# Two hybrid layers on one core: weaving the last second product by fifths, a norm in two stages, weights loaded in pieces

## The chip, the core and the metric

The kernel runs on one core of a Trainium2 chip. The core has TensorE (PE, matmuls; PEld is its weight load), VectorE (DVE), ScalarE (ACT), GpSimd (POOL) and SyncE (SP), which here issues nearly all DMAs. The metric is the device time of one execution in microseconds, lower is better.

## The reference

Two pairs of a linear-attention layer and a dense layer run one after the other over x of shape 1 x 2048 x 576, in float32, with the same weights in both pairs:

```python
def _A_ref(x, wqkv, w_phi, wo):                 # H = 32 heads of Dh = 18
    qkv = (x @ wqkv) ...                        # q, k, v
    pq, pk = q @ w_phi, k @ w_phi               # per head
    phi_q = concat(softmax(pq), softmax(-pq)); phi_k = the same of pk
    kv = phi_k^T v;  z = sum of phi_k over the sequence
    o = (phi_q kv) / (phi_q z + 1e-6)
    return o @ wo
def _B_ref(x, w1, b1, w2, b2):                  # F = 4608
    return relu(x @ w1 + b1) ** 2 @ w2 + b2
for both pairs:
    x = x + _A_ref(layernorm(x), ...)
    x = x + _B_ref(layernorm(x), ...)
```

The sums kv and z go over the whole sequence, so no query of a layer can be finished before all keys of that layer are through.

## The kernel before

**Tiles.** The sequence is cut into four blocks of TB = 512 rows, each of NT = 4 tiles of 128. To keep float32's accuracy each operand of a large matmul is held as a high part (F32R, a rounded copy made on ScalarE) and a low part (what is left, subtracted on VectorE or GpSimd), and a product is the sum of three: high by high, high by low, low by high. A projection of one tile and one half of the 576 columns (`project`, L476 to 485) is 14 matmuls of 288 columns; `make_v` (L487) and `make_raw` do both halves of a tile one after the other. `kv_tile` (L558) adds a tile to the sums kv in 64 small matmuls (as the trace counts them) of 36 columns.

**Order of the work.** The program is Python that is traced; a planner then orders each engine's instructions by their place in the source and by when it thinks their inputs are ready, and takes buffers from pools. The kernel steers it by generators that `yield` costs: `weave(main, other, rate)` (L101) adds `rate` for every step of `main` and pays steps of `other` from it. `tc.issue_after(ins)` keeps what is traced inside it, on the engine of `ins`, behind `ins` in that engine's queue; it is an order and no wait. `held` (L668) and `chained` (L129) wrap generators in it: `chained` keeps each step's VectorE, ScalarE and GpSimd instructions behind those of the step before. Buffers matter too: work woven beside a product has two PSUM buffers (tag w), x tiles have five, weights of the kind q, k, v or o two for each part (whi, wlo).

**Stages.** `g_fold` (L233) folds w_phi into the q and k weights and splits the k and v weights (in its inner `times`, ScalarE and GpSimd split v's chunk c at L302 and L303 as soon as chunk c is folded). Keys and values of layer 0 follow. Then in each layer:

- `barrier` (L1384): the queries of two blocks, the end of the sums, and for the first block the features of its queries. `g_phi` (L715) goes tile by tile: products with z (`phi_products`, one on VectorE, one on GpSimd, L694), sums (L700), factors, scaling (L712). Two tiles are finished, tile 2's products are begun, and `g_out` (L743) is called with two parts: part 0 turns tiles 0 and 1 (L768) and multiplies them by kv (L784). The rest of `g_phi`, so tile 3's products too, comes behind the last subtraction of part 0 (L788). Then come the output projections (`x_after`, L794, matmuls at L805), part 1, and `g_norm`, which makes the normed and transposed input of the dense layer: `moments` (L370) computes statistics on VectorE (L375, L376) and the reciprocal root on GpSimd (L377, L378), `scale` applies them (L393, L394), and `transpose`, `split_main`, `transpose_rest`, `split_rest` (L404 to L426) turn tiles and split them. `keep` (L827) adds the second bias on GpSimd and stores the row tile.
- two blocks through `g_mlp` (L846), with the attention of other blocks woven in (`back_first` at rate 3.7, `back_second` at 5.0);
- the last two blocks as a pair in `g_pair`: `products` (w1, by a scheme with fewer block products) and one block's second product (w2); then `seconds` (L1339) does the other block's second product: per f of NF = 36, `by_rows` is 12 matmuls of 448 columns (L1231), `features` is 3 of 512 (L1221), with loads of w2 (L1188) and of the hidden rows hd (L1269) three f ahead. In layer 0 `back_keys` (L1496), the norm, v, k and sums of the next layer's first three blocks, is woven into `seconds` at rate 4.0. Its norm is `g_norm` with `fine=True`: four tiles scaled one after the other, 2.2 each, then turned and split.

Once split, a weight is stored to DRAM (`keep_split`) and later loaded as it is: `wloaded` (L354) loads both parts of a half at once by `moved` (L346); `wpair` takes both halves.

The stages that the change touches are the fold, the barrier, the loads of q and o, and `back_keys` inside `seconds`. The weave around `seconds` is this:

```python
        back = iter(()) if layer else chained(back_keys())
        for k, _ in enumerate(products):
            if k == NP - 1:
                next(back, None)
                next(back, None)
        weave(seconds, back, 4.0)
```

## Time and profile before

| | us |
|---|---|
| three timed runs: median (lowest to highest) | 2530.28 (2529.72 to 2532.84) |
| the profiled execution, its own time | 2538.57 |
| span of its instructions | 2536.8 |
| TensorE's mean granted clock over the span | 0.992 |

The profile comes from one execution, which took a little longer than the timed runs; its times count from the first instruction. Rows show instructions by line, engine and tile, the output's name before the arrow; buffer numbers are left out, and a block's number stands in the name: n_3, n_2 and n_0 are the norms that `back_keys` makes for blocks 3, 2 and 0 (and those names serve layer 0's norms too), w_3k0h is the high part of half 0 of the k weights loaded for block 3, t0 and t1 are the barriers of layers 0 and 1, m_pacacc and m_pach the sums of `seconds`. A row of waits names the waiting engine, tile and line, what it waited for, then the time in total, the number of waits, and the longest. Ends of matmuls are modelled, so the distance between starts says more than a matmul's own duration.

### The profile page before, as it was taken

To read this page: it belongs to the slowest core of one execution; us is meant where nothing else is said; L and a number is where in the kernel's file an instruction comes from. 1 tells how busy PE (TensorE), PEld (TensorE's weight loads), DVE (VectorE), ACT (ScalarE), POOL (GpSimd) and SP (SyncE) were. 2 spreads that over 40 slices of the span, in tenths; PEclk is the share of its full clock that TensorE was granted. 3 is DMA by queue.
4 is the path that set the end of the run, shared out by engine and by line. 5 is a ranking of instruction groups with operands and counts; after the bars stand their busy time and mean duration, and the time that the engine had idled before them with its cause. 6 is when DMAs were issued, how large, how long until landed. Compare 5 with 4: busy or idle time off the path is not lost.

```text
span 2536.8 us, 41468 instructions
## 1 busy us (share of the span) xinstructions
PE 2481.7 (98%) x15108; PEld 2179.8 (86%) x15108; DVE 1570.9 (62%) x2514; ACT 1265.5 (50%) x2245; POOL 949.5 (37%) x1101
## 2 busy tenths in 40 slices
PE   8998999999999999999999989999999999999999
PEld 8997888889888888888889988888898888888888
DVE  6778848554856655554667679394548566555444
ACT  4344545443446666663333435454445466666642
POOL 3544312212325555551333333031123355565322
PEclk8999999999999999999999999999999999999999
DMA  9222643356434433328654134333563444333363
GB/s 326 79 69 91 196 116 85 103 164 213 133 119 125 143 114 99 113 93 295 206 180 148 47 128 150 102 99 98 166 222 112 129 130 142 116 96 109 112 199 127
DMA packets 249691, 348.52 MB, mean 137 GB/s; under 512 B 30158, under 2 KB 157262, under 8 KB 246926
## 3 DMA queue, kind: packets, MB, share of 16 engines
q1 hardware_dynamic: 248228, 343.18, 42.7%
q8 instruction: 118, 1.93, 0.3%
q10 hardware_dynamic: 1258, 2.70, 0.3%
q14 instruction: 87, 0.71, 0.1%
HBM read 279.46 MB, written 66.32 MB: 136 GB/s over the span
## 4 chain that ended last, share of the span: by engine, by line
PE 47%; DVE 3%; DMA 2%; ACT 1%; POOL 1%; issue 1%; SPq 0%; DVEq 0%; ACTq 0%; POOLq 0%
PE m_1ph L887 5%; PE m_0ph L887 4%; PE m_pacacc L1231 4%; PE m_ppx L1202 4%; PE m_1acc L914 3%; PE m_0acc L914 3%; PE m_pacc L1231 3%; PE m_ppy L1202 2%; PE m_pacacc L1221 2%; PE m_pach L1231 1%; PE m_0acc L905 1%; PE m_1acc L905 1%; PE m_pacc L1221 1%; PE m_ppz L1202 1%; PE a_0po L805 1%
## 5 line engine op out<-in xcount | busy, mean ns | idle before, releaser
L1192 POOL TENSOR_TENSOR m_ps<-m_pr,m_ps 128x128 fp32r<-128x128 f32 x144 | 118.2, 821 | 338.6 <-ACT m_ps L1190 282.9
L1191 DVE TENSOR_TENSOR m_ps<-m_pr,m_ps 128x448 fp32r<-128x448 f32 x144 | 98.1, 681 | 194.7 <-ACT m_ps L1190 191.3
L1231 PE MATMUL m_pacc<-m_ps,m_phb 128*128 128x448 f32 x864 | 188.5, 366 | 0.0
L1231 PEld LDWEIGHTS m_pacc<-m_ps,m_phb 128*128 128x128 f32 x864 | 162.2, 188 | 18.0
L1190 ACT ACTIVATE m_ps<-m_pr 128x576 fp32r<-128x576 f32 x144 | 98.1, 681 | 154.5 <-issue 88.2
L1231 PE MATMUL m_pacacc<-m_ps,m_phc 128*128 128x448 f32 x648 | 147.7, 370 | 0.0
L1231 PEld LDWEIGHTS m_pacacc<-m_ps,m_phc 128*128 128x128 f32 x648 | 122.6, 190 | 9.9
L1212 DVE TENSOR_TENSOR m_phb<-m_pz,m_phb 128x512 fp32r<-128x512 f32 x72 | 56.5, 784 | 113.1 <-ACT m_pz L1211 111.6
L914 PE MATMUL m_2acc<-m_2s,m_2hb 128*128 128x448 f32 x432 | 100.2, 366 | 0.0
L914 PE MATMUL m_0acc<-m_0s,m_0hb 128*128 128x448 f32 x432 | 100.1, 366 | 0.0
L887 PE MATMUL m_3ph<-t0onh,m_3h 128*128 128x512 f32 (+1 forms) x380 | 98.0, 383 | 1.6 <-DVE t0onh L426 0.8
L914 PE MATMUL m_1acc<-m_1s,m_1hb 128*128 128x448 f32 x432 | 99.4, 365 | 0.0
L914 PE MATMUL m_3acc<-m_3s,m_3hb 128*128 128x448 f32 x432 | 99.4, 365 | 0.0
L887 PE MATMUL m_1ph<-t1onh,m_1h 128*128 128x512 f32 (+1 forms) x380 | 97.8, 382 | 1.5 <-DVE t1onh L426 0.8
L887 PE MATMUL m_0ph<-a_0nh,m_0h 128*128 128x512 f32 (+1 forms) x380 | 97.8, 384 | 0.0
L887 PE MATMUL m_2ph<-a_2nh,m_2h 128*128 128x512 f32 (+1 forms) x380 | 97.8, 384 | 0.0
L914 PEld LDWEIGHTS m_2acc<-m_2s,m_2hb 128*128 128x128 f32 x432 | 80.9, 188 | 10.5 <-ACT m_2hb L895 0.2
L914 PEld LDWEIGHTS m_0acc<-m_0s,m_0hb 128*128 128x128 f32 x432 | 80.9, 188 | 10.6 <-ACT m_0hb L895 0.2
L914 PEld LDWEIGHTS m_1acc<-m_1s,m_1hb 128*128 128x128 f32 x432 | 81.1, 188 | 10.3
L914 PEld LDWEIGHTS m_3acc<-m_3s,m_3hb 128*128 128x128 f32 x432 | 81.1, 188 | 10.3
L872 POOL TENSOR_TENSOR m_3s<-m_3r,m_3s 128x128 fp32r<-128x128 f32 x36 | 24.6, 683 | 168.6 <-ACT m_3s L867 154.1
L872 POOL TENSOR_TENSOR m_1s<-m_1r,m_1s 128x128 fp32r<-128x128 f32 x36 | 24.7, 686 | 167.7 <-ACT m_1s L867 153.3
(2440 smaller groups left out, 7372.1 us busy)
## 6 DMA issues: line engine op xcount, KB each, us to landing
m_pr<-in_B_w SPq DMA_DIRECT2D x144, 288.0 KB
m_pr<-in_B_w SPq DMA_DIRECT2D x72, 256.0 KB
hd<-m_pu SPq DMA_DIRECT2D x72, 256.0 KB
m_pg<-hd SPq DMA_DIRECT2D x72, 256.0 KB
m_3r<-in_B_w SPq DMA_DIRECT2D x36, 288.0 KB
m_2r<-in_B_w SPq DMA_DIRECT2D x36, 288.0 KB
m_1r<-in_B_w SPq DMA_DIRECT2D x36, 288.0 KB
m_0r<-in_B_w SPq DMA_DIRECT2D x36, 288.0 KB
```

The lines of the kernel that those rows point to most:

```text
L805: nc.tensor.matmul(pt[:, :HP], a, m[:w, g], start=(g == 0 and k == 0), stop=(g == NG - 1 and k == 2))
L872: nc.gpsimd.tensor_sub(s2[:, D + R : 2 * D], r2[:, R:], s2[:, R:D].bitcast(F32))
L887: dense["hidden"] = nc.tensor.matmul(ph[:, cols], a, m, start=(k == 0), stop=(k == len(ops) - 1))
L905: nc.tensor.matmul(acc[KC], a, m, start=(f == 0 and k == 0), stop=(f == NF - 1 and k == 2))
L914: nc.tensor.matmul(acc[t][:, :R], a[:, rows], m, start=(f == 0 and k == 0), stop=(f == NF - 1 and k == 2))
L1190: nc.scalar.activation(s2[:, :D], r2, AF.Copy)
L1191: nc.vector.tensor_sub(s2[:, D : D + R], r2[:, :R], s2[:, :R].bitcast(F32))
L1192: nc.gpsimd.tensor_sub(s2[:, D + R : 2 * D], r2[:, R:], s2[:, R:D].bitcast(F32))
L1202: nc.tensor.matmul(ps, a, m, start=start and i == 0, stop=i == len(ms) - 1, skip_group_check=True)
L1212: nc.vector.tensor_sub(hl, r, hh.bitcast(F32))
L1221: nc.tensor.matmul(accs[b][KC], a, m, start=(g == 0 and k == 0), stop=(g == NF - 1 and k == 2))
L1231: nc.tensor.matmul(accs[b][t][:, :R], a[:, rows], m, start=(g == 0 and k == 0), stop=(g == NF - 1 and k == 2))
```

## The change

- **By fifths, in TensorE's source order.** `seconds` yields after each tile's row matmuls and after the features, five times per f, and the rate is 0.85 (it was one yield at 4.0). `chained(..., strict=True)` also keeps each woven step's matmuls behind the last matmul traced before it.
- **The norm in two stages.** With `fine=True`, `begin` (the load and the statistics) of tile t+1 is a step of its own ahead of `scale` of tile t. Six such steps of the first block are taken before the last step of `products` ends (there were two steps of one tile each). The next block's first six are taken between the half projections of v.
- **Weights in pieces.** `g_load` issues one part of one half per step, each behind SyncE's last traced DMA. v is projected half by half (`half_v`) and k's halves are loaded after each; q and o are loaded in such steps too.
- **The barrier.** `g_phi` goes away: products and sums of tiles 2 and 3 are both traced before `g_out`, their GpSimd part behind GpSimd's last traced instruction. In `g_out` with two parts, the tail is written out: norm tiles 0 and 1 behind part 1's last subtraction, transposes behind named output projections, bias additions and stores behind the last needed root.
- **The fold.** v's chunk c is split when chunk c+1 is folded, the last two together.

```diff
-    def chained(gen):
+    def chained(gen, strict=False):
         ends, engines = {}, (nc.vector.engine, nc.scalar.engine, nc.gpsimd.engine)
         while True:
             traced = nc.cur_bb.bb.instructions
             mark = len(traced)
+            if strict:
+                ends[nc.tensor.engine] = traced_on(nc.tensor)
...
+            for c in ([c - 1] if i == 2 and c else []) + ([c] if i == 2 and c == KC else []):
                 for half in range(2):
                     hi, lo = (piece[:, c] for piece in vpair[half])
...
+    def g_load(which, half, name, into):
+
+        into[half] = piece_tiles(f"{name}{which}{half}", TAGS_A)
+        for p in range(2):
+            with tc.issue_after(traced_on(nc.sync)):
+                moved(which, half, into[half], False, (p,))
+            yield 1.0
...
-        for t in range(NT):
-            apart(t)
-            yield 2.2
-        yield from pipeline(3 * NT // 2, (cross, split), (0.3, 0.6))
+        yield from pipeline(NT, (start, apart), (2.0, 1.6))
+        yield from pipeline(3 * NT // 2, (cross, split), (0.3, 0.9))
...
+        scale, turn_rows, turn_rest = next(g_norm(xs_of.__getitem__, dst, f"{name}n", None, None))
...
+        with tc.issue_after(dense["part"].ins):
+            xns = [scale(t) for t in range(2)]
+        xs_of.append(x_after(2))
+        behind_out(turn_rows, 0, xns[0])
+        other = g_after(3)
+        next(other)
+        behind_out(turn_rows, 1, xns[1])
+        behind_out(turn_rest, 0)
+        xs_of.append(next(other))
+        xns.append(scale(2))
+        kept_rows(0, 1)
+        behind_out(turn_rows, 2, xns[2])
+        xns.append(scale(3))
+        kept_rows(2, 3)
+
+        def rest():
+            turn_rows(3, xns[3])
+            turn_rest(1)
...
-                second(f)
+                for t in range(NT):
+                    by_rows(f, [t], range(3))
+                    yield
+                features(f, range(3))
+                del high[f], wide[f]
                 yield
...
         def own():
-            yield from g_q(x, wpair("q", name), raws, name)
+            pair = {}
+            for half in range(2):
+                yield from g_load("q", half, name, pair)
+            yield from g_q(x, pair, raws, name)
...
-        next(phi)
+        with tc.issue_after(traced_on(nc.gpsimd)):
+            for t in range(2, NT):
+                add(t)
+        phi = (finish(t) for t in range(2, NT))
...
+                for n, cost in enumerate(norm):
+                    yield cost
+                    if n > 5:
+                        next(loads, None)
+                drain(loads)
...
                 if not last:
                     spill(b, xk)
-                    yield from paced(g_v(xk, wpair("v", f"w{m}"), vts, f"v{m}"), 1.0)
-                pair = wpair("k", f"w{m}")
+                    norm = norm_of(order[i + 1])
+                    vts = [next_slot() for _ in range(NT)]
+                    for half in range(2):
+                        for t in range(NT):
+                            half_v(xk, t, wv[half], half, vts[t], f"v{m}")
+                            yield 0.5
+                            if len(ahead) < 6:
+                                ahead.append(t)
+                                yield next(norm)
+                        yield from paced(g_load("k", half, f"w{m}", wk), 0.3)
+                    ahead.clear()
...
                 yield from pipeline(NT, (raw, start, lambda t: soft_exp(es[t]), end, keep_sums),
-                                    (1.0, 2.6, 0.4, 1.8, 0.8))
+                                    (0.5, 2.4, 0.4, 2.0, 0.8))
...
-        back = iter(()) if layer else chained(back_keys())
+        back = iter(()) if layer else chained(back_keys(), True)
         for k, _ in enumerate(products):
             if k == NP - 1:
-                next(back, None)
-                next(back, None)
-        weave(seconds, back, 4.0)
+                for _ in range(6):
+                    next(back, None)
+        weave(seconds, back, 0.85)
```

More of the change, by code (lines that the diff above doesn't have):

```diff
@@ L344, in parts_of, with moved @@
         return [(slice(0, P), 0, NC)]
-    def moved(which, half, pair, back):
-        for piece, home in zip(pair, wsplit[which]):
+    def moved(which, half, pair, back, only=(0, 1)):
+        for i in only:
+            piece, home = pair[i], wsplit[which][i]
             for p, c0, c1 in parts_of(which):
@@ L824, in g_out @@
             yield from mid
-        pair = pair or pieces()
         def keep(t, x):
@@ L1426, in barrier, with add, finish @@
         spare["tags"] = [f"acc{i}" for i in range(NC)] + ["h"]
-        phi = g_phi(layer, er, ph, f"{n}f")
-        for _ in range(4):
-            next(phi)
-            next(queries)
+        us = {}
+        def add(t):
+            us[t] = phi_sums(phi_products(layer, er[t][0], f"{n}fm{t}", "x"), f"{n}fu{t}")
+        def finish(t):
+            phi_factors(us.pop(t), er[t][1])
+            phi_scale(*er[t])
+            ph.append(er[t][0])
+        for step, t in ((add, 0), (finish, 0), (add, 1), (finish, 1)):
+            step(t)
+            next(queries, None)
             next(queries, None)
@@ L1497, in back_keys, with norm_of @@
             new_slots("vs")
-            late = []
-            for b in order[:3]:
+            late, ahead = [], []
+            normed = {b: {} for b in order[:3]}
+            def norm_of(b):
+                return g_norm(rows_of(b), normed[b], f"n1_{b}", fine=True)
+            norm = norm_of(order[0])
+            for i, b in enumerate(order[:3]):
                 m = f"1_{b}"
                 last = b == order[2]
-                xk, vts, raws, es, rs = {}, [], {}, {}, {}
-                yield from g_norm(rows_of(b), xk, f"n{m}", fine=True)
+                xk, vts, raws, es, rs = normed[b], [], {}, {}, {}
+                wv, wk = {}, {}
+                which, ready = ("k", wk) if last else ("v", wv)
+                loads = (cost for half in range(2) for cost in g_load(which, half, f"w{m}", ready))
+                for n, cost in enumerate(norm):
+                    yield cost
+                    if n > 5:
+                        next(loads, None)
+                drain(loads)
                 while late:
```

84 lines of the change are left out of this document (46 added, 38 removed).

## The prediction

> **What bounds the kernel now.** I read the page's first part, then the sums of busy time over stretches of the span, then TensorE's waits in the stretches the change touches.
>
> ```profile
> span 2536.8 us, 41468 instructions
> PE 2481.7 (98%) x15108; PEld 2179.8 (86%) x15108; DVE 1570.9 (62%) x2514; ACT 1265.5 (50%) x2245; POOL 949.5 (37%) x1101
> ```
>
> TensorE is the bound: 98% busy, VectorE next with 62%. The change removes no matmul, so it can only win back TensorE's idle and slowed time. Where that is, the stretches tell (first columns: length, PE busy; PEclk is the granted clock):
>
> ```profile
> core 0: us, PE busy (x) PEld busy (x) DVE busy (x) ACT busy (x) POOL busy (x), PEclk, DMA share, GB/s
> 0.00:50.00 50.00, 40.85 (x260) 38.47 (x261) 30.77 (x83) 20.55 (x53) 16.93 (x44) 0.86 0.96 317
> 200.00:265.00 65.00, 53.02 (x390) 50.39 (x389) 52.74 (x105) 22.86 (x56) 30.22 (x28) 0.95 0.41 140
> 265.00:1147.00 882.00, 878.77 (x4308) 751.72 (x4307) 531.55 (x841) 486.15 (x843) 335.77 (x415) 1.00 0.41 128
> 1163.10:1386.20 223.10, 207.61 (x1678) 190.41 (x1677) 139.32 (x201) 80.44 (x139) 75.35 (x75) 0.96 0.60 203
> 1455.00:1520.00 65.00, 58.25 (x497) 55.81 (x496) 51.03 (x109) 24.95 (x59) 25.04 (x24) 0.97 0.39 129
> 1520.00:2537.00 1017.00, 1009.60 (x4924) 866.61 (x4922) 591.02 (x924) 535.53 (x924) 364.83 (x438) 1.00 0.43 132
> ```
>
> Three touched stretches hold the loss: layer 0's last second product, 1163.1 to 1386.2, is idle for 223.1-207.6 = 15.5 us, and its clock of 0.96 costs another 4% of 223.1 = 8.9 us; the two barriers (200 to 265, 1455 to 1520) are idle for 12.0 and 6.8 us. Layer 1's second product, part of 1520 to 2537, has nothing woven into it and full clock.
>
> I check the stage by what its matmuls need: rows of the chain of work, and of TensorE's timeline.
>
> ```profile
> 2422.67 1.84 PE m_pacacc L1231 x9
> 2425.81 1.84 PE m_pacacc L1231 x9
> 1262.70 14.74 PE v_2pv L484 x112
> ```
>
> ```profile
> 1229.40 0.77 PE L573 MATMUL kvp<-k_3K0e,vs 128*32 128x36 f32 x64
> 1230.11 0.88 PE L1231 MATMUL m_pach<-m_ps,m_phc 128*128 128x448 f32 x3
> 1244.53 1.04 PE L404 MATMUL n_2p<-ident,n_2n 128*128 128x128 f32 x8
> 1245.33 0.85 PE L1231 MATMUL m_pach<-m_ps,m_phc 128*128 128x448 f32 x3
> ```
>
> One f of the product takes 2425.81-2422.67 = 3.14 us, 36 of them 113.0. A block's v or k projection takes 14.74, and there are five: 73.7. A state update takes 1230.11-1229.40 = 0.71, eight of them 5.7; eight transposes take 0.80, so 60 take 6.0. Sum 198.4 of 223.1: 24.7 us are lost, and 15.5+8.9 = 24.4 says the same.
>
> **The change part by part.** *The woven product.* TensorE's waits in this stretch:
>
> ```profile
> PE n_2p L418 <- DVE n_2l L413: 6.1, 1, 6.1
> PE n_0p L418 <- DVE n_0l L413: 5.6, 1, 5.6
> PE k_3kp L484 <- DMA w_3k0h<-wskh: 1.9, 1, 1.9
> PE n_3p L418 <- DVE n_3l L413: 1.8, 1, 1.8
> ```
>
> Norms are 13.5 of 15.4. They start late (after the block before is through), and VectorE, in order, stands at each tile for GpSimd's reciprocal root, so the split that frees a PSUM buffer comes late. After the change three of a block's four tiles are normed beside the block before's v projection: six norm steps against eight half projections. The first block gets three tiles before the product begins, instead of two. Splitting start and apart lets tile t+1's statistics fill the wait of tile t. I take the 13.5 as gone, and with it the slow clock that follows stalls: 8 of 8.9.
>
> Half weights come later and pinned: v and k each load by half, k's first half under v's second half's four tiles (4 x 1.84 us plus woven work), its second only after v is done. The landing seen is
>
> ```profile
> 1192.64 6.21 DMA w_3k0h<-wskh
> ```
>
> so 6.21 us from issue. Cover for a second half: the first half's projection of one tile, 14.74/8 = 1.84, and about 0.5/0.85 fifths of 0.63. Uncovered that leaves some 4 us, unless product matmuls already stand ahead in TensorE's queue, as in k_2kp's case, where no wait was seen. The second and third block's first half is asked for late too (after the norm's seventh remaining step). For ten half loads the exposure lies between 0 and 10 x 6.21 = 62; I take 4.5 us, near the 1.9 that one block shows, three times, less what it was. Two things are queued behind a late half: on SyncE, where its load waits for the buffer of an earlier half, the product's own hd and w2 loads, which run three f (9.4 us) ahead, so that their splits on ScalarE and VectorE, and then TensorE, wait only for longer delays; on TensorE, which is in order, everything.
>
> Budget of the weave, in the planner's cost units. Before: a norm 8.8+5.4, v 4.0, k 26.4, a late update 0.8, less two steps taken ahead, in three blocks 40.2+45.4+41.4 = 127.0 of 35 x 4.0 = 140. Now: a norm 14.4+7.2 of which 10.8 is taken ahead, v with the next norm's steps and k's loads 16.0, k 24.4, so 51.2+52.0+36.0 = 139.2 of 35 x 5 x 0.85 = 148.75. Back work ends (148.75-139.2)/4.25 = 2.2 f before the product's end instead of 3.2, still covered. Term: -13.5-8+4.5 = **-17**, bounds -24.7 and +37.
>
> *The barriers.* Waits in the first and in the second:
>
> ```profile
> PE t0opt L768 <- DVE t0fQ1e L712: 3.5, 1, 3.5
> PE t0onp L404 <- DVE t0onn L393: 2.3, 3, 1.3
> PE kt L631 <- DVE kq L625: 2.2, 1, 2.2
> PE t0opt L768 <- DVE t0fQ0e L712: 1.2, 1, 1.2
> PE t0opt L768 <- DVE t0fQ3e L712: 0.9, 1, 0.9
> PE m_3ph L887 <- DVE t0onh L426: 0.8, 1, 0.8
> PE m_3ph L887 <- ACT t0onh L412: 0.7, 1, 0.7
> ```
>
> ```profile
> PE t1onp L404 <- DVE t1onn L393: 2.3, 3, 1.3
> PE t1opt L768 <- DVE t1fQ1e L712: 2.0, 1, 2.0
> PE t1opt L768 <- DVE t1fQ3e L712: 0.9, 1, 0.9
> PE m_1ph L887 <- DVE t1onh L426: 0.8, 1, 0.8
> ```
>
> The norm's waits are 2.3+0.8+0.7 = 3.8 in each. Part of them is GpSimd's queue:
>
> ```profile
> 246.40 1.42 POOL L828 TENSOR_TENSOR t0ox<-t0ox,b2t 128x576 f32<-128x576 f32 x1 [0.92 <-DVE t0one L394]
> 247.79 0.21 POOL L377 TENSOR_SCALAR t0ond<-t0onm 128x1 f32<-128x1 f32 x1
> ```
>
> The bias addition (1.42) stands ahead of the next tile's statistics. The change queues these additions (and SyncE's stores of xm, read only after the dense block) behind the last needed root, and transposes behind output projections of 30 matmuls that are ready. I take 3.5 of 3.8, twice: -7.0. With tile 3's products and sums ahead of part 0, the wait for t0fQ3e goes: -1.8 for both. What this puts ahead on VectorE, where TensorE already waits for Q1:
>
> ```profile
> L694 DVE TENSOR_TENSOR t0fm<-t0fQ2e,zb 128x576 f32<-128x576 f32 x1 | 1.7, 1685 | 0.0
> L700 DVE TENSOR_REDUCE t0fu<-t0fm 128x32 f32<-128x576 f32 x8 | 5.8, 734 | 0.0
> L694 DVE TENSOR_TENSOR t0fm<-t0fQ3e,zb 128x576 f32<-128x576 f32 x1 | 0.7, 747 | 0.0
> ```
>
> One product and two sums, 0.75+2 x 0.73 = 2.2 us, or 3.2 where the product takes 1.69 as Q2's. GpSimd's products now queue behind Q1's scaling, which helps Q1. All of it on the path twice: +6.4; all Q1, Q0 and kq waits gone: -8.9. I take +0.3. Behind the moved products stand the copies of part 0's transposes. Term: -7.0-1.8+0.3 = **-8.5**, bounds -18.7 (12.0+6.8) and +6.4.
>
> The 1685 and 747 ns of one shape show a contest. The Trainium skill, SBUF — State Buffer, section "Who interferes with whom", says that a VectorE instruction with two SBUF inputs and a GpSimd one that reads SBUF lock each other out for a whole instruction; the rows agree. It speaks against moving two GpSimd products to where VectorE is busiest; by it each of four moved products could add about 1 us more (an estimate from the two rows), and the barrier term would be -4.5.
>
> *The fold at the start* defers one chunk's ScalarE and GpSimd splitting of v.
>
> ```profile
> PE n_0p L404 <- DVE n_0n L393: 2.5, 1, 2.5
> PE fp L270 <- ACT ff L285: 1.4, 1, 1.4
> ```
>
> The second wait had v's copies ahead on ScalarE. Bounds: -3.9 (both gone) and +2.0 (v's last two chunks late for the first projection); I take **-0.5**, since the start moves 317 GB/s and waits elsewhere too.
>
> *q and o in pieces.* Each query stage gets four more steps of cost 1.0; o's loads ride on the turns. The same transfers, behind SyncE's last traced one. Cover: from 265 to 1147 TensorE idles 3.2 of 882 us. I take **0**; -2 to +6 (one landing of 6.21 uncovered).
>
> Sum -17-8.5-0.5 = -26. The profiled execution took 2538.6 (span 2536.8 and 1.8 around it), so it would give 2512.6; the three timed runs' median is 8.3 lower, 2530.3, hence **2504 us**.
>
> **The rivals.** *A: more than that.* All 24.7 and half of the 18.8 in the barriers: -34, 2496 and below. For it: stretches with steady weaving idle 0.4%. Against: the planned order must fit the chip's delays everywhere.
>
> *B: half of the stage.* The norm now holds three of the five x buffers when the first product half ends and takes four for its residual; where those loads come late, the sums leave PSUM late and the second half's first matmuls wait, and norm steps beside v hold up the copies that free v's PSUM. Stage -6, barriers -6: 2518.
>
> *C: nothing.* The edge added on TensorE holds back steps behind product matmuls, but nothing holds product matmuls back; the queue may come out much as before, and the barriers' gain of 8.5 be eaten by 6.4 on VectorE: about 2528.
>
> *D: slower, by SyncE's queue.* SyncE's own waits in the stage:
>
> ```profile
> SPq L1188 <- DVE m_ps L1191: 89.3, 25, 10.5
> ```
>
> SyncE stands 89.3 of 223 us ahead of a w2 load whose buffer isn't free, and weights now queue behind such loads, in source order, near their use. If all ten half loads are then exposed by e, the cost is 10e against 26+4.5 = 30.5 saved: it decides at e = 3.05 us. At e = 4.5 the time is 2530.3+14.5 = 2545. Against: 6.21 is a landing at a crowded time, and fifths of the product can fill.
>
> **How the numbers follow.** Forecast (2497 to 2512) 0.45; A 0.12; B (2512 to 2525) 0.20; C 0.06; D 0.17. Within 0.2%, 5 us, about what a measurement of this kernel can tell from no change, lies C. Faster 0.77, same 0.06, slower 0.17. The range reaches from 2490, into A, to 2530, through B and most of C.
>
> **What would show it.** Right: no wait over 1 us for the norms' splits in the stage, its clock at 0.99 or more, the stage at 200 to 210 us, the waits for t0onn, t1onn and Q3 gone. Wrong: new waits for w halves by DMA (D), waits for Q1 longer than 3.5 and 2.0 (barrier term), the first product matmul on acc0 waiting for the residual's load (B), or idle time between 265 and 1147 above 3.2 (the pieces).

## The result and the profile after

The change makes the kernel slightly slower: 2536.06 us (median; 2533.28 to 2541.21) against 2532.27 us for the kernel before, run beside it on the same chip. The ratio is 1.0017, 95% interval 1.0010 to 1.0025. The forecast was 2504 us (2497 to 2512); the result lies above its range.

The profiled execution of the changed kernel took 2536.06 us, its median. The one of the kernel before took 2538.57, some 6 us more than its own median; so the two spans (2536.8 and 2534.3) differ by -2.5 us where the timed runs differ by +3.8. I therefore compare stretch by stretch, and over several executions where I can.

The page's first part, after:

```profile
span 2534.3 us, 41473 instructions
PE 2480.5 (98%) x15108; PEld 2178.4 (86%) x15108; DVE 1573.4 (62%) x2514; ACT 1268.5 (50%) x2245; POOL 952.9 (38%) x1101
```

TensorE is as busy as before. The stretches of the span that the prediction looked at (columns as there; the barriers and the stage begin some us earlier or later, because what lies ahead of them has moved):

```profile
core 0: us, PE busy (x) PEld busy (x) DVE busy (x) ACT busy (x) POOL busy (x), PEclk, DMA share, GB/s
200.00:270.00 70.00, 54.70 (x382) 52.20 (x381) 54.19 (x103) 21.49 (x53) 30.19 (x28) 0.88 0.34 111
270.00:1147.00 877.00, 871.61 (x4272) 746.11 (x4271) 530.86 (x839) 483.68 (x837) 334.74 (x413) 1.00 0.42 127
1173.90:1378.86 204.96, 202.59 (x1678) 185.78 (x1677) 131.89 (x195) 81.02 (x139) 75.46 (x73) 1.00 0.65 223
1455.00:1520.00 65.00, 54.89 (x390) 52.19 (x390) 49.60 (x104) 23.38 (x56) 23.06 (x23) 0.92 0.31 101
```

The woven stage takes 204.96 us instead of 223.1 (first `m_pach` matmul to first `v_prev` matmul on TensorE's timeline), at full clock and with 2.4 us idle. What it won is lost elsewhere: the first barrier is idle for 15.3 us instead of 12.0 and its clock is 0.88 instead of 0.95, the second for 10.1 instead of 6.8 at 0.92 instead of 0.97, and the long stretch behind the first barrier for 5.4 instead of 3.2.

TensorE's waits in the stage, after:

```profile
PE n_0p L436 <- DVE n_0l L431: 1.5, 1, 1.5
PE k_3kp L506 <- ACT m_ps L1237: 0.5, 1, 0.5
PE n_2p L436 <- DVE n_2l L431: 0.2, 1, 0.2
```

The norm splits' 13.5 us have shrunk to 1.7; one of them is still over the 1 us that the forecast allowed. TensorE's waits in the first barrier, after:

```profile
PE t0opt L786 <- DVE kbl L634: 3.9, 1, 3.9
PE t0opt L786 <- DVE t0fQ1e L741: 2.5, 1, 2.5
PE m_3ph L934 <- DVE t0ox L826: 2.5, 1, 2.5
PE t0onp L422 <- DVE t0onn L411: 1.4, 1, 1.4
```

and in the second:

```profile
PE t1opt L786 <- DVE kbl L634: 4.8, 1, 4.8
PE m_1ph L934 <- DVE t1onh L444: 2.1, 2, 1.3
PE t1onp L422 <- DVE t1onn L411: 1.3, 1, 1.3
PE t1opt L786 <- DVE t1fQ1e L741: 0.8, 1, 0.8
```

The wait for Q3 is gone and that for Q1 is 1.0 and 1.2 us shorter. In their place stands a wait that the prediction did not have, 3.9 and 4.8 us, for `kbl`: the low part of the last group of kv, whose subtraction frees the PSUM buffer of `kt`. And the norm's waits have not gone, as the forecast had it; a new one, for `t0ox`, stands at the first matmul of the dense block.

**Why kbl is late.** VectorE's instructions, after (start, duration, line, output and input; in brackets the idle time before and what ended it), GpSimd's beside them, and kbl before:

```profile
218.82 0.75 DVE L729 TENSOR_REDUCE t0fu<-t0fm 128x32 f32<-128x576 f32 x1 [1.30 <-POOL t0fm L723]
219.50 1.82 DVE L723 TENSOR_TENSOR t0fm<-t0fQ3e,zb 128x576 f32<-128x576 f32 x1
222.60 0.75 DVE L729 TENSOR_REDUCE t0fu<-t0fm 128x32 f32<-128x576 f32 x1 [1.29 <-POOL t0fm L723]
223.27 0.29 DVE L634 TENSOR_TENSOR kbl<-kt,kbh 72x144 fp32r<-72x144 f32 x1
```

```profile
216.87 1.92 POOL L723 TENSOR_TENSOR t0fm<-t0fQ2e,zb 128x576 f32<-128x576 f32 x1
219.17 1.53 POOL L915 TENSOR_TENSOR m_3h<-m_3r,m_3h 128x640 fp32r<-128x640 f32 x1
220.66 1.91 POOL L723 TENSOR_TENSOR t0fm<-t0fQ3e,zb 128x576 f32<-128x576 f32 x1
```

```profile
219.69 0.29 DVE L605 TENSOR_TENSOR kbl<-kt,kbh 72x144 fp32r<-72x144 f32 x1
```

VectorE works in order. Tile 2's sums (L729) stood ahead of kbl before, too; now tile 3's product and one of its sums stand there as well. Two of these sums need a product that GpSimd makes, and GpSimd makes both late: tile 2's behind the scaling of Q1 (at 216.87 us; before it was made ahead of that scaling, at 214.52), tile 3's behind a split of the next block's w1 (L915). VectorE stands idle twice, 1.30 and 1.29 us; the added work of its own, a product of 1.82 us and a sum of 0.75, takes as long again. So kbl comes 3.6 us later although the first turned features came 0.6 us earlier. The slow clock that follows makes it dearer. TensorE's stretch at half clock here, after and before:

```profile
215.80:229.50 13.70, 8.06 (x36) 7.45 (x37) 9.53 (x17) 3.93 (x11) 8.68 (x7) 0.50 0.46 130
```

```profile
216.30:223.10 6.80, 3.94 (x19) 3.95 (x20) 5.62 (x11) 1.92 (x5) 5.90 (x7) 0.50 0.10 31
```

Among the runs below, this stretch lasts 13.7 to 17.1 us in the four executions with the new denominators (after, e3, e4, e6) and 6.8 to 10.2 us in the thirteen others.

**Why the norm's tail did not get shorter.** Two scalings of one tile, after; the bias additions that GpSimd does at that time; and the same scaling before:

```profile
254.44 1.61 DVE L411 TENSOR_SCALAR t0onn<-t0ox,t0onm,t0ond 128x512 f32<-128x512 f32 x1 [0.67 <-POOL t0ond L393]
255.98 1.43 DVE L412 TENSOR_SCALAR t0one<-t0ox,t0onm,t0ond 128x128 f32<-128x128 f32 x1
```

```profile
254.38 2.95 POOL L853 TENSOR_TENSOR t0ox<-t0ox,b2t 128x576 f32<-128x576 f32 x2
```

```profile
248.69 0.55 DVE L393 TENSOR_SCALAR t0onn<-t0ox,t0onm,t0ond 128x512 f32<-128x512 f32 x1 [1.44 <-POOL t0ond L378]
```

Two additions wait for the last needed root and then start with the scaling that the same root released. The scalings take 1.61 and 1.43 us instead of 0.55 and 0.34; they end 0.3 and 0.1 us behind an addition's end.

**o's weights.** One of the long stretches, `back_second` of layer 0 (first `m_2ph` to first `m_ppx` matmul), is 308.5 us instead of 304.2. SyncE asks for o's weights of block 1 there at 696 us instead of 642; its row after, and before:

```profile
696.35 0.78 SPq L359 DMA_DIRECT2D a_1o0h<-wsoh  x2
```

```profile
642.26 1.54 SPq L352 DMA_DIRECT2D a_1o0h<-wsoh  x2
```

My theory after this reading: the product's new weave does what it should, worth 16 to 18 us of the profile; the **denominators** (sums of tiles 2 and 3 ahead of part 0), the **norm's tail** and the **pieces** (o's late loads) each cost time. The main rival: the parts only move the slack around, so that undoing one changes nothing. The experiments undo or add one part at a time.

### The profile page after: what moved, and what is told of

The parts are those of the page before. It is cut to its first block, busy times and chain, and to the rows that moved or that the text cites. A ratio compares the mean times of both kernels' runs of the same rounds, so it can differ in the third digit from the quotient of the medians.

```text
span 2534.3 us, 41473 instructions
## 1 busy us (share of the span) xinstructions
PE 2480.5 (98%) x15108; PEld 2178.4 (86%) x15108; DVE 1573.4 (62%) x2514; ACT 1268.5 (50%) x2245; POOL 952.9 (38%) x1101
## 4 chain that ended last, share of the span: by engine, by line
PE 85%; DVE 6%; DMA 3%; ACT 2%; POOL 2%; issue 1%; SPq 1%; DVEq 0%; ACTq 0%; POOLq 0%
PE m_ppx L1249 8%; PE m_pacc L1278 6%; PE m_pacacc L1278 5%; PE m_1ph L934 5%; PE m_3ph L934 5%; PE m_0ph L934 4%; PE m_ppy L1249 4%; PE m_2ph L934 3%; PE m_3acc L961 3%; PE m_1acc L961 3%; PE m_0acc L961 3%; PE m_2acc L961 3%; PE m_pacacc L1268 2%; PE m_pach L1278 2%; PE m_pacc L1268 2%; PE m_ppz L1249 2%
## 5 line engine op out<-in xcount | busy, mean ns | idle before, releaser
L1238 DVE TENSOR_TENSOR m_ps<-m_pr,m_ps 128x448 fp32r<-128x448 f32 x144 | 96.7, 672 | 178.9 <-ACT m_ps L1237 173.9
L1237 ACT ACTIVATE m_ps<-m_pr 128x576 fp32r<-128x576 f32 x144 | 98.1, 681 | 123.8 <-issue 71.6
L961 PE MATMUL m_3acc<-m_3s,m_3hb 128*128 128x448 f32 x432 | 99.5, 365 | 0.0
```

Source lines behind the costliest of these rows:

```text
L961: nc.tensor.matmul(acc[t][:, :R], a[:, rows], m, start=(f == 0 and k == 0), stop=(f == NF - 1 and k == 2))
L1237: nc.scalar.activation(s2[:, :D], r2, AF.Copy)
L1238: nc.vector.tensor_sub(s2[:, D : D + R], r2[:, :R], s2[:, :R].bitcast(F32))
```

## The experiments

Tables first, since the texts refer to them. Times are medians; each ratio is to the kernel before, run beside it. Columns of the second table are distances between the first matmuls of two names on TensorE's timeline of one profiled execution: the *stage* is `m_pach` to `v_prev`; the *barriers* are `t0opt` to `m_3acc` plus `t1opt` to `m_1acc` (in brackets the part up to `t0onp` and `t1onp`, the first transposes of the norm); *back* is `m_2ph` to `m_ppx` in layer 0, and `m_0ph` to `m_ppx` in layer 1.

| run | what it is | us | ratio (95%) |
|---|---|---|---|
| after | the change | 2536.06 | 1.0017 (1.0010, 1.0025) |
| e1 | weave and fold only | 2520.22 | 0.9957 (0.9945, 0.9970) |
| e2 | the change with the old denominators | 2530.07 | 1.0000 (0.9991, 1.0008) |
| e3 | the change with the old tail | 2531.57 | 1.0006 (0.9997, 1.0015) |
| e4 | the change with q and o loaded whole | 2534.86 | 1.0011 (1.0001, 1.0021) |
| e6 | e1 with the new denominators, kbl ahead of their sums | 2530.34 | 0.9996 (0.9987, 1.0005) |
| e8 | e1 with the new tail, bias additions last | 2516.77 | 0.9946 (0.9933, 0.9960) |
| e9 | e1, tile 3's products early | 2522.46 | 0.9957 (0.9944, 0.9971) |
| e10 | e1, no norm beside v | 2532.49 | 1.0005 (0.9996, 1.0014) |
| e11 | e1, woven by whole f | 2520.05 | 0.9964 (0.9951, 0.9977) |
| e12 | e1, old norm and loads: fifths alone | 2533.80 | 1.0006 (0.9998, 1.0015) |
| e13 | e8 with q and o in pieces | 2523.90 | 0.9970 (0.9960, 0.9980) |
| e14 | e8 with q in pieces | 2522.11 | 0.9958 (0.9946, 0.9971) |
| e15 | e8 with o in pieces | 2528.99 | 0.9991 (0.9982, 1.0000) |
| e16 | e8 again | 2519.03 | 0.9945 (0.9932, 0.9959) |

| run | stage | barriers (to the norm) | back 0 | back 1 |
|---|---|---|---|---|
| before | 223.2 | 98.0 (59.7) | 304.2 | 304.6 |
| e5, before again | 220.2 | 97.1 (59.0) | 304.4 | 305.8 |
| after | 205.0 | 109.3 (66.6) | 308.5 | 303.7 |
| e1 | 205.9 | 98.1 (60.0) | 304.8 | 304.2 |
| e2 | 206.3 | 104.0 (59.3) | 308.0 | 306.4 |
| e3 | 206.8 | 105.7 (67.5) | 306.6 | 306.4 |
| e4 | 206.1 | 110.4 (67.8) | 303.9 | 304.2 |
| e6 | 205.5 | 109.5 (70.9) | 304.2 | 304.0 |
| e8 | 205.4 | 97.1 (58.8) | 304.2 | 304.0 |
| e9 | 205.8 | 98.0 (59.9) | 303.7 | 308.2 |
| e10 | 220.7 | 95.8 (57.7) | 305.0 | 305.2 |
| e11 | 207.5 | 96.0 (57.8) | 304.5 | 304.1 |
| e12 | 223.0 | 97.3 (58.7) | 304.3 | 303.9 |
| e13 | 206.0 | 96.4 (59.4) | 304.5 | 306.1 |
| e14 | 206.5 | 97.5 (59.3) | 305.7 | 304.3 |
| e15 | 206.3 | 96.7 (59.7) | 309.5 | 309.6 |
| e16 | 205.9 | 99.5 (60.0) | 304.4 | 305.4 |

### e1: the weave and the fold alone

Denominators, tail and the loads of q and o go back to what they were:

```diff
-        with tc.issue_after(traced_on(nc.gpsimd)):
-            for t in range(2, NT):
-                add(t)
-        phi = (finish(t) for t in range(2, NT))
+        next(phi)
...
-        with tc.issue_after(dense["part"].ins):
-            xns = [scale(t) for t in range(2)]
...
+        norms = (norm or g_norm)(x_next, dst, f"{name}n", keep)
...
-            for half in range(2):
-                yield from g_load("q", half, name, pair)
-            yield from g_q(x, pair, raws, name)
+            yield from g_q(x, wpair("q", name), raws, name)
```

> Only the woven second product and the fold of the change; the barrier and the loads of q and o as before. Theory: the weave gains what the first profile shows (stage 204.97 instead of 223.15 us, 18.2), of which the timed runs keep about 11, because the profiled execution of before was 6.3 us over its median; the barriers (+6.4 and +4.8) and o's loads (+4.2) took it back. So stage 203 to 207 us, barriers back at 50.3 and 47.8 (from the first transposed features to the first second-product matmul), and the whole at -10 to -13 us, ratio 0.995 to 0.996. Rival, the weave's gain was an accident of one slow execution of before: ratio 0.998 to 1.001.

Measured: 2520.22 us, 10.7 under before and 15.8 under the change. The barriers are back at 98.1, the stage stays at 205.9.

### e2, e3, e4: the change without one part

e2 undoes the denominators (the first part of the diff above), e3 the tail (the second), e4 the pieces of q and o (the third, and o's twin).

> The change with the denominators of tiles 2 and 3 put back in tile order; all else as changed. Theory: the waits for kbl (3.9 and 4.8 us) go, the part of the barriers from the first transposed features to the first transposed norm falls from 34.7 and 31.9 to 30.8 and 28.9, the whole by 6.9 us: ratio to before 0.998 to 1.000. Rival, that the stretched part comes from the new tail of the output projections, which starts in the same stretch: no fall there, ratio 1.001 to 1.003.

> The change with the norm's old tail in the barrier (additions of the second bias and transposes where they stood); all else as changed. Theory: the part of the barriers from the first transposed norm to the first second-product matmul falls from 22.0 and 20.7 to 19.5 and 18.9 us, the whole by 4.4: ratio to before 0.9995 to 1.001. Rival, that this part is late only because the denominators push it: no fall, ratio 1.001 to 1.003.

> The change with q's and o's weights loaded as before, all four at once; all else as changed. Theory: the o weights of layer 0's last block are asked for at about 642 us again instead of 696 to 703, the wait of TensorE for a_1fh (1.8 us) and the half clock after it go, the stretch from m_2ph to m_ppx falls from 308.5 to 304.2 us, ratio to before 0.999 to 1.001. Rival, that this stall is an accident of that one execution: stretch at 308, ratio 1.001 to 1.003.

Measured: with the old denominators, 2530.07 us and barriers of 104.0 instead of 109.3; ahead of the norm they win even 7.3 us (59.3 instead of 66.6). With the old tail, 2531.57 us and 105.7; behind the norm's start the distances fall from 42.7 to 38.2. Without the pieces, back 0 is 303.9 instead of 308.5, but the time, 2534.86, has an interval that overlaps the change's. So denominators and tail each lengthen their own part of the barrier, and do not only move slack. In time, the interval of e2 lies apart from the change's, and that of e3 still touches it. A later pair settles the tail: e13 differs from e2 only in the place of the bias additions, and has a ratio of 0.9970 instead of 1.0000 and barriers of 96.4 instead of 104.0. The pieces stayed unclear here.

### e5: the kernel before, profiled again

> The kernel before, unchanged, profiled in another execution. If the difference between its first profiled execution (2538.57 us) and its timed median (2532.3) lies in single late loads and not in the stage, its woven stage is again near 223 us, the distances from the first transposed features to the first transposed norm are again near 30.8 and 28.9 us, and back_second of layer 0 again near 304 us. If instead the stage itself differs from one execution to the next, it comes out several us shorter, and the 17 to 18 us that the profiles show for the weave are partly chance.

Measured: a stage of

```profile
1161.06:1381.28 220.22, 206.76 (x1678) 190.16 (x1677) 139.34 (x201) 80.70 (x139) 75.86 (x75) 0.97 0.61 205
```

220.2 us in an execution of 2532.94 us: 2.9 less than in the first profile, the barriers 0.9 less. So some 3 of the 18 us by which the stage shrank in the first pair of profiles were that one execution's. This lies between what the two theories gave.

### e6: the new denominators, but kbl ahead of the sums

```diff
-            nc.vector.tensor_sub(lo, own, hi.bitcast(F32))
+            dense["kbl"] = nc.vector.tensor_sub(lo, own, hi.bitcast(F32))
...
-        with tc.issue_after(traced_on(nc.gpsimd)):
+        with tc.issue_after(traced_on(nc.gpsimd)), tc.issue_after(dense["kbl"].ins):
             for t in range(2, NT):
                 add(t)
```

> The weave and the fold as in the change, the tail, o and q as before, and the denominators of the last two tiles first as in the change, but with the last group's low part (kbl, which frees kt) traced ahead of those tiles' VectorE products and sums. Theory: what costs is that VectorE, in order, stands behind sums that wait for GpSimd's products; with kbl ahead the wait only moves on to the copies of the turned features, and the distance from t0opt to t0onp stays at 33 to 35 us (layer 1: 32 to 33.5), the time within 3 us of 2530. Rival: only kbl's place behind the sums costs; then the distances fall to 30 to 31 and 28.5 to 29 us, and the time to 2520 or lower.

Measured: 2530.34 us, barriers 109.5 (70.9 ahead of the norm, more than in the change; its parts, 36.3 and 34.6, are a little over the ranges expected). TensorE's waits, first and second barrier:

```profile
PE t0opn L802 <- DVE t0of L789: 6.7, 1, 6.7
```

```profile
PE t1opn L802 <- DVE t1of L789: 7.6, 1, 7.6
```

The wait moved to the first thing that stands behind the sums now, the copies of the turned features. So it is not kbl's place that costs, but that VectorE stands, in order, behind work that GpSimd feeds:

```profile
218.52 1.41 DVE L729 TENSOR_REDUCE t0fu<-t0fm 128x32 f32<-128x576 f32 x2 [3.62 <-POOL t0fm L723]
```

### e9: only the products early

```diff
+        add(2)
+        ms = phi_products(layer, er[3][0], f"{n}fm3", "x")
+
+        def rest_phi():
+            finish(2)
+            us[3] = phi_sums(ms, f"{n}fu3")
+            finish(3)
+            yield
+
+        phi = rest_phi()
```

> The weave and the fold as in the change, tail, o and q as before, and of the new order of the denominators one half: tile 3's two products stand ahead of part 0, but its sums behind it, so that nothing that TensorE needs stands on VectorE behind a GpSimd product. Theory (sums in front of needed work are the cost, not GpSimd's products being earlier): t0opt to t0onp 29.5 to 31, layer 1 28 to 29.3 us, the wait for t0fQ3e (0.9 us each) shorter or gone, time 2518 to 2521. Rival (GpSimd's products next to VectorE's cost by themselves, whatever stands behind them): the distances are 32 or more and 30.5 or more, the time 2524 to 2530.

Measured: barriers 98.0 as in e1, and 2522.46 us with the same ratio as e1. GpSimd's products being earlier costs nothing by themselves, and gains nothing that can be measured: of the wait for Q3 nothing is left, but in the first and the second barrier TensorE waits a little for kbl instead:

```profile
PE t0opt L786 <- DVE kbl L634: 0.5, 1, 0.5
```

```profile
PE t1opt L786 <- DVE kbl L634: 1.4, 1, 1.4
```

### e8: the new tail with the bias additions last

```diff
-        kept_rows(0, 1)
         behind_out(turn_rows, 2, xns[2])
         xns.append(scale(3))
-        kept_rows(2, 3)
...
             turn_rest(1)
+            kept_rows(0, 1, 2, 3)
```

> The weave and the fold as in the change, denominators, o and q as before, and the change's norm tail, but with the four bias additions on GpSimd and their stores behind the whole norm. Theory: in the change's tail the additions (1.4 us each) collide with VectorE's scaling, so the distance from t0onp to the first matmul of the dense block (22.0 us in the change, 19.3 with the old tail; layer 1 20.7 and 18.9) falls to 19.5 and 18.9 or less, while t0opt to t0onp stays at 30.2; the time comes to 2515 to 2520. Rival: the additions are not the cause but the order in which VectorE is given scaling, copies and splits; then the distance stays at 21.5 to 22.7 and 20.5 to 22.7 us and the time at 2523 to 2526.

Measured: the distances from the norm to the dense block are 19.84 and 18.41 us (22.0 and 20.7 in the change), so it was the additions, as the theory said; 19.84 is a little over its bound of 19.5. A rest of the collision is left: the additions still start with the last root, and the last tile's scaling takes

```profile
253.47 1.63 DVE L411 TENSOR_SCALAR t0onn<-t0ox,t0onm,t0ond 128x512 f32<-128x512 f32 x1 [0.42 <-POOL t0ond L393]
```

But in the whole barrier the tail won nothing either. The seven executions with the old tail and the old place of the sums (before, e5, e1, e9, e10, e11, e12) have barriers of 95.8 to 98.1, mean 97.2; the five with this tail (e8, e13 to e16) 96.4 to 99.5, mean 97.4. From the norm to the dense block, the ten distances with this tail fall into two groups, by the clock. Where it stayed full they are 18.6 us in the first barrier and 18.4 in the second, less than in the seven with the old tail (19.2 to 19.7, and 18.9). In four of the ten TensorE was granted half clock for 3.4 us, and they are 19.7 to 19.8; with the old tail no execution (those seven, e3 and e6) has half clock there. The waits for `t0onn` fell from 2.3 to 0.3 us in e8's first barrier, and other waits took their place at the dense block's first matmuls:

```profile
PE m_3ph L941 <- DVE t0ox L837: 1.4, 1, 1.4
PE m_3ph L941 <- DVE t0onh L444: 0.8, 1, 0.8
PE m_3ph L941 <- ACT t0onh L430: 0.7, 1, 0.7
PE t0onp L422 <- DVE t0onn L411: 0.3, 1, 0.3
```

Why these waits bring half clock in e8 and the same ones don't in e13 is open.

### e10, e11, e12: what in the weave earns the gain

The edge that `strict` adds on TensorE needed no run: the built program is the same with and without it. The other parts were taken apart on e1. e10 takes no norm step beside v:

```diff
-                            if len(ahead) < 6:
+                            if len(ahead) < 0:
```

e11 weaves by whole f:

```diff
-                for t in range(NT):
-                    by_rows(f, [t], range(3))
-                    yield
-                features(f, range(3))
-                del high[f], wide[f]
+                second(f)
                 yield
...
-        weave(seconds, back, 0.85)
+        weave(seconds, back, 4.25)
```

e12 keeps the fifths and has the old norm, the old loads and two steps ahead:

```diff
-        yield from pipeline(NT, (start, apart), (2.0, 1.6))
+        for t in range(NT):
+            start(t)
+            apart(t)
+            yield 2.2
...
-                    for half in range(2):
-                        for t in range(NT):
-                            half_v(xk, t, wv[half], half, vts[t], f"v{m}")
...
+                    yield from paced(g_v(xk, wpair("v", f"w{m}"), vts, f"v{m}"), 1.0)
+                pair = wpair("k", f"w{m}")
```

> As e1_weave_only, but no step of the next block's norm is taken between v's half projections: only the first block keeps its six steps ahead. Theory (norms that start only after the block before is through make TensorE stand at n_2 and n_0): the stage m_pach to v_prev goes from 205.9 to 212 to 219 us, with waits of 3 us or more for the splits of n_2 or n_0, the time to 2526 to 2531. Rival (the fifths alone spread the work enough): the stage stays at 204 to 208 us and the time at 2518 to 2522.

> As e1_weave_only, but the product is woven by whole f (one yield per f at rate 4.25) instead of fifths; norm in two stages, norm beside v and pieces of weights stay. Theory (the norms' place earned most, the fifths the cover of late halves): the stage is 207 to 213 us, without waits of 3 us for norm splits, but with short waits at the projections; time 2521 to 2527. Rival (the fifths earned the gain): the stage is 216 to 223 us, the time 2527 to 2532.

> The product by fifths at 0.85 and the fold as in the change; the norm, v, k and their loads inside the stage as before (one step of one tile, whole weights, two steps ahead), all else as before. Theory (the norms' place earned the gain): the waits at n_2 and n_0 stay at 3 us or more each and the stage at 215 to 222 us, time 2527 to 2532. Rival (the fifths earned it): the stage is 204 to 210 us, time 2518 to 2523.

Measured: without the norm beside v the stage is 220.7 us, even more than expected: nearly the whole gain is gone. Fifths alone: 223.0, no gain. Whole f with all the rest: 207.5, 1.6 more than e1, at a time that can't be told from e1's (2520.05 and 2520.22 us). TensorE's waits in the stage, e10, e11 and e12 in this order:

```profile
PE n_0p L436 <- DVE n_0l L431: 4.2, 1, 4.2
PE n_2p L436 <- DVE n_2l L431: 4.1, 1, 4.1
PE k_2kp L506 <- DMA w_2k1h<-wskh: 2.6, 1, 2.6
```

```profile
PE k_2kp L506 <- DMA w_2k1h<-wskh: 2.0, 1, 2.0
PE k_3kp L506 <- DMA w_3k1h<-wskh: 1.9, 1, 1.9
PE n_0p L436 <- DVE n_0l L431: 0.5, 1, 0.5
```

```profile
PE n_2p L436 <- DVE n_2l L431: 5.9, 1, 5.9
PE n_0p L436 <- DVE n_0l L431: 5.3, 1, 5.3
PE k_3kp L509 <- DMA w_3k0h<-wskh: 2.2, 1, 2.2
```

Norming the next block beside the block before's v projection earns the stage's gain; the fifths only cover the late second halves of k (3.9 us of waits in e11). Whether norm steps beside v would do it without the two-stage norm and the pieces was not tried.

### e13 to e16: the pieces of q and o

e13 has both on e8's base, e14 q's alone, e15 o's alone, e16 is the base again, run beside e14 and e15. o's part:

```diff
-        loads = iter(())
-        pair = pieces()
-        keep_split("o", pair)
+        pair, loads = {}, iter(())
+        if "o" in kept and parts == 1:
+            loads = (cost for half in range(2) for cost in g_load("o", half, name, pair))
```

> As e8_bias_last, and the loads of q and o in pieces as in the change. Theory (o's pieces come 50 us later, into a stretch whose transfers are full, and make a w1 load late): back_second of layer 0, m_2ph to m_ppx, goes from 304.2 to 306 to 309 us, with a wait of 1 us or more behind a hidden row's eviction and a clock below 0.97 in 700 to 730 us; the time comes to 2518 to 2521, 2 to 4 us over e8_bias_last. Rival (late loads there are chance, as the executions of before show them elsewhere too): 304 to 305 us and a time within 1.5 us of e8_bias_last's 2516.8.

> As e8_bias_last, with q alone loaded in pieces. Theory (o's late loads are the cost): the time is within 2 us of e16_base_again. Rival (q's pieces, which put four more steps of cost 1.0 into each query stage and so shift the steps behind them, are the cost): 4 to 8 us over e16_base_again, with the loss in the back stages of both layers, m_2ph to m_ppx and m_0ph to m_ppx.

> As e8_bias_last, with o alone loaded in pieces during the turns. Theory: 4 to 8 us over e16_base_again, with TensorE waiting for evictions (a_1fh, a_2fh) behind late w1 loads in m_2ph to m_ppx or in m_0ph to m_ppx, a stretch of 304 us otherwise. Rival (q's pieces, or neither): within 2 us of e16_base_again.

> e8_bias_last unchanged. If e8's 2516.8 us was no chance, the time is 2515 to 2519 and both back_second stretches are 303.5 to 304.8 us; if e8 was a lucky set of runs, the time is 2520 to 2523 and e13's pieces cost 1 to 4 us, not 7.

e13 came to 2523.90, 7 us over e8's median, but its profile showed 304.5 in back 0: the theory's place was not there, which is why e14 to e16 followed. With o's pieces alone the time is 2528.99, 10 us over e16, with intervals that do not touch, and the back stretches are 309.5 and 309.6. What happens there in layer 0 (waits of ScalarE, then of TensorE; then 680 to 700 us of e15, and of e16):

```profile
ACT m_2h L923 <- DMA m_2r<-in_B_w: 3.8, 1, 3.8
```

```profile
PE a_1pn L813 <- DVE a_1fl L800: 3.7, 1, 3.7
```

```profile
680.00:700.00 20.00, 16.31 (x71) 13.48 (x71) 9.91 (x16) 7.41 (x13) 3.16 (x3) 0.91 0.90 227
```

```profile
680.00:700.00 20.00, 19.95 (x97) 16.89 (x96) 14.66 (x24) 9.76 (x17) 4.65 (x5) 1.00 0.40 115
```

The four o loads fall among the loads of w1, the DMA engines are 90% busy, a w1 load is late, and ScalarE, in order, stands 3.8 us at its split. Behind it stand the copies of the turned features, and TensorE waits 3.7 us for those. So it isn't o's own weights that come late, but others that queue beside them. With q alone the time is 3 us over e16, but the intervals overlap; with both it is some 6 over the base by the ratios, less than with o alone. Why q's pieces lessen o's price is open; in e13's profile the DMA engines are 92% busy from 690 to 700 us and yet the wait at a_1pn is 0.4 us, so the price seems to depend on how o's loads happen to fall among w1's. Nor does such a stall need the pieces: in e9, with o loaded whole, ScalarE stands 3.8 us for a w1 load in back 1, TensorE waits 2.9 us behind it, and the stretch takes 308.2. But of the ten back stretches with o in pieces eight are over 306 us, of the 24 without it only that one.

The base itself repeated: 0.9946 and 0.9945, though e16's 2519.03 us and its back 1 of 305.4 lie a little over what was expected. It beats before by 0.5% and the change by 0.7%, but its interval and that of e1 overlap, so whether the new tail adds anything to the weave is not settled; the barriers say that it does not.

## Why the prediction was wrong

**The woven product: -17. Right.** The stage takes 205.0 to 206.8 us in the twelve executions with the whole weave (e11's whole f apart), mean 206.0, and 220.2 to 223.2 in the four without norm beside v, mean 221.8: -15.8. The norm waits went, but for 1.7 us, and the clock is 1.00, as forecast. That the sum came out so near is partly luck, since two of its terms were too large and offset each other. The late halves cost less than the 4.5 taken (1.6 in e16; in the change only 0.5 at `k_3kp`, put down to a split). And the slow clock cost less than 8.9: at full clock TensorE is busy for 202.6 us of the stage, so of the 207.6 us before, the slow clock made 5.0. The prediction charged the clock to the idle time as well, and its 198.4 us of needed work, which seemed to confirm that, is 4 short of what all the executions at full clock show. What did not come over in full is the time: e1, e8, e9 and e16 are 10 to 15 us under before, 12 on the mean, not 16. The other distances vary by a few us from one execution to the next (the barriers of unchanged code by 2.3), and I could not settle where the rest goes.

**The barriers: -8.5. Wrong in sign, and this is the step that failed.** The change's two executions with both new parts (after, e4) have barriers of 109.3 and 110.4, against 97.2 with the old code: +12.6. Two sentences carry it.

- "I take +0.3" for what is put ahead on VectorE. The prediction counted VectorE's own work (2.2 to 3.2 us) and noted, rightly, that Q1 gets earlier (1.0 and 1.2 us). It did not follow the products that the sums need: GpSimd makes them, behind Q1's scaling and among the w1 splits, so that in the first barrier VectorE idles 2.6 us in front of the next needed instruction, on top of its own work. It also named only the copies as what stands behind, and missed kbl. With the half clock that follows, the price is 8.5 us (e3 against 97.2) to 12.3 us (e6) for both barriers, above the bound of +6.4, which held VectorE's work alone.
- "I take 3.5 of 3.8" for the norm, twice. Reordering around GpSimd's queue moved the bias additions beside VectorE's scalings, which they stretch from 0.55 and 0.34 to 1.61 and 1.43. e2 has this alone: barriers of 104.0, +6.8 instead of -7.0. Even without the collision (e8, e13 to e16) the tail gains some 0.5 to 0.7 us in a barrier where the clock stays full, not 3.5, and loses as much or more where half clock follows: taking out one wait showed the next.

For the products the prediction had weighed a rule that bears on this, too. The row: a scaling with one tensor input takes 1.61 us beside GpSimd's addition and 0.55 without. The Trainium skill, SBUF — State Buffer, section "Who interferes with whom", also lists `tensor_scalar` among the VectorE operations that can enter a two-port mode; in that mode they contend with GpSimd, and the one that issues first blocks the other for the whole instruction. The trace agrees: the additions begin 0.06 and 0.25 us ahead of the scalings, which end 0.3 and 0.1 us behind them; the mode itself no row shows. I had used that section for the products only. There the contest just changed tiles (1.69 and 0.75 us for the products of tiles 2 and 3 before, 0.69 and 1.82 after). In e9 both are contested (1.69 and 1.84), at no cost that can be measured.

**q and o in pieces: 0. Too low, within its bounds.** The ten back stretches with o in pieces have a mean of 306.9 us, the 24 without 304.6: 4.6 us for the two layers; the timed runs of e15, o alone, show 10. In the first half of these dense blocks, q's pieces show 268.5 and 268.9 us in e14 (`m_3acc` to `m_2ph`, `m_1acc` to `m_0ph`), against 268.2 in both in e16, another 1.1. "TensorE idles 3.2 of 882 us" was taken as cover. It says that nothing was late there, not that there was room: when o's loads stood among w1's, the DMA engines were 90% busy in e15 and a w1 load came late. The sign that the prediction named for this did come: 5.4 us idle in that stretch.

**The fold: -0.5. Can't be told.** The time to the first v matmul is 36.9 and 35.4 us without it, 34.5 to 39.2 with it.

The sum by the profiles: -15.8 + 12.6 + 4.6 + 1.1 = +2.5, near the +3.8 timed. Of the rivals, C came nearest in time, with about 2528 us. It had the barriers' gain eaten by VectorE, rightly, but it wrongly had the product unchanged. D, the one that ended slower, at 2545, named SyncE's queue in the stage; in the change TensorE has no wait for a weight's load there.

## What to carry to other kernels

Before work is moved ahead on an in-order engine, follow each of its inputs to the engine that makes it and ask when that engine gets there: the moved instructions' own durations are only a part of the price (here about half of kbl's delay), and what is next needed behind them pays. A wait that a view names is worth its length only if no other stands close behind it, so list what comes next in the chain first. Charge a slow clock to busy time alone; a stretch's idle time is already counted. Start work for the next block beside the one before's long projection, which here earned nearly all that the finer weaving was given the credit for, and ask for weights at times when the transfers have room, not just before use.

## What the hardware showed that I had not expected

- A 1.4 us addition on GpSimd that had begun just before stretched a VectorE scaling of 128x512 from 0.55 to 1.61 us, and the next addition one of 128x128 from 0.34 to 1.43; the statistics and the sums out of PSUM beside GpSimd's additions in the kernel before (0.40 to 0.46 us) were not stretched.
- TensorE stayed at half clock for 13.7 us in the first barrier, though it was busy for 8.06 of them; a second wait, of 3.9 us, stands in the middle. Executions without such a wait had 6.8 to 10.2 us there.
- Four loads of 567 KB and as many of 81 KB, asked for beside the w1 loads, went with 90% DMA share and a w1 load so late that ScalarE stood 3.8 us (e15); asked for 38 us earlier (e16) they went with 63%, and no such wait followed.
